# VectorE operations on two tiles at once, chained shifts and a different share of key tiles in a hand-scheduled attention block on one core

## The chip, the core and the metric

The kernel runs on one core of a Trainium2 chip. The core's engines are TensorE (PE, matmuls; its weight loads appear as PEld), VectorE (DVE), ScalarE (ACT), GpSimd (POOL) and SyncE (SP), which here only starts DMAs. The metric is the device time of one execution in microseconds (us); lower is better.

## The reference

```python
B, S, D, H = 1, 2048, 448, 16          # Dh = 28
qkv = (x @ wqkv).reshape(B, S, 3, H, Dh).transpose(2, 0, 3, 1, 4)
q, k, v = qkv[0], qkv[1], qkv[2]
scores = jnp.einsum("bhqd,bhkd->bhqk", q, k) * (Dh ** -0.5)
p = softmax(scores, axis=-1)
o = jnp.einsum("bhqk,bhkd->bhqd", p, v)
return o.transpose(0, 2, 1, 3).reshape(B, S, D) @ wo
```

All tensors are bfloat16. It is one multi-head self-attention block: projections, softmax(q k) v for 16 heads of 28 columns over 2048 positions, and an output projection.

## The kernel before

**Units and tiles.** The 16 heads are taken in four groups of four, the 2048 queries in four chunks of 512. A pair of group and chunk is a unit; there are 16. Inside a unit the keys come in 16 tiles of 128. For one unit, key tile and head the scores are a tile of 128 keys by 512 queries, one PSUM bank of float32. So there are 1024 score tiles. They come out of L911 (`s_one`): four heads lie in four row groups of 32 rows, so that matmuls of different heads can run side by side. The weighted sum over keys (L863, `pv_mm`) puts the four heads into four column groups of one accumulator bank; one pass over one key tile is four matmuls. An additional column of ones in the values yields the softmax's denominators. No maximum is subtracted; a check of the denominators at the end of the program (CK..., FLAG) chooses a general path (`_general`) if they leave a range.

**Two ways to an exponential.** The exponential is shared between two engines.

- *A tiles* go to ScalarE. Two score tiles form a group, held in banks 0 and 1 or, for the next group, 2 and 3. One ACTIVATE (L952) reads both and writes the bf16 weights into PT, a ring of 38 tiles. PE then makes one pass for each key tile (`pv_a`).
- *D tiles* go to VectorE. The score has been scaled so that one binary order is 1024 units. L972 (the operation named R) adds a constant, clips at zero and writes an int16, whose bits read as float16 are a piecewise linear version of the exponential. This first plane is written for four heads into PD[zs, 0]. Two shifted copies of it are made by L978 (H1, plus 341) and L980 (H2, plus 683), each an operation on 128x2048 int16 values. PE passes over all three planes with three differently weighted copies of the values (VC, factors TERM_C), three passes of four matmuls in place of one, and the sum of the three lines is much closer to the exponential (`pv_d`). PD has four slots (NZ = 4).

`D_COUNT` says for each unit how many of its 16 key tiles go to VectorE: 75 of 256 in all. `D_SETS` says which.

**Banks.** Banks 4 to 7 are a pool called M. From it come the accumulators of the units, the banks of projections, of output projections, and the banks of the D tiles, one for each. A D tile's bank is released by its R.

**Other work on the way.** The projections of keys, queries and values (L550, L572) are made while the units run and are evicted by VectorE (L532, L534). GpSimd writes the values and their weighted copies in place (L585, L591). When a unit is complete, `post_unit` evicts its accumulator to OTS (L730), takes the denominators through DRAM and back (L733 to L742), inverts them (L737), and GpSimd multiplies in four quarters of 128 queries (L747, `NM`), which puts the normalised output into QT. When all four head groups of a chunk are there, `out_proj` makes four output tiles (L698), evicts them (L712) and stores them by a DMA from SP (L714). The last unit has its own ending, `tail`: the first three head groups of its output projection are made ahead (L775, `PREOP`), the denominators are taken across partitions by small matmuls (L797, L810) instead of through DRAM, the fourth head group is added (L821), and four tiles are evicted, two by ScalarE (L824) and two by VectorE (L827), and stored (L829).

**Order.** All operations are first collected with their dependencies and a nominal duration. Then a planner (`_Prog.schedule`) simulates the engines once while the program is built and so fixes a static order for each engine: it takes the engine with the earliest possible start and, among the operations that can start within 150 ns, the one of the lowest `prio`. R has priority -90, evictions -95 to -100, shifts the running position. A D tile's score matmul rides along with the score matmuls of an A group if it can (`ride`, L156); otherwise it waits up to RIDE ns for it. `HOLD_BACK` lets a group's scores wait for a bank that comes free soon. On the chip every engine goes through its list in order, and an operation waits on semaphores for those that it depends on (`emit_engine`), also for those of its own engine. An operation that waits holds up everything behind it on its engine.

## Time and profile before

The median of five runs is 354.24 us (353.55 to 354.87). The profiled execution took 354.13 us; its span in the profile, first to last instruction, is 352.2 us.

| operation | line | count | mean ns of one |
|---|---|---|---|
| exponential of two A tiles, ScalarE | L952 | 362 | 1233 |
| R, one D tile, VectorE | L972 | 300 | 681 |
| H1, H2, one shift, VectorE | L978, L980 | 75 + 75 | 708, 712 |
| eviction of K and Q projections, VectorE | L534, L532 | 16 + 15 | 684, 685 |
| eviction of a unit's accumulator, VectorE | L730 | 15 | 681 |
| eviction of an output tile, VectorE | L712 | 12 | 611 |
| normalisation of 128 queries, GpSimd | L747 | 60 | 560 |

```profile
PE   7899999999999999999999999999999899999995
PEld 3333232223322232322322232332222222222223
DVE  1788999999999999999999998999999999999974
ACT  1899999999999999999999999999999999999991
```

How to read it: the span is cut into 40 equal slices, and each digit is the busy share of a slice in tenths, 9 being 90% or more. A mean duration contains latency that overlaps with the next instruction, so means times counts can be more than an engine's busy time. A row of a group ends with the idle time of the engine just before these instructions and what ended it. A chain row says when a stretch began, how long it took and which engine and line it was on. A row of waits reads: who waited for whom, us in total, times, longest.

### The profile page before, as it was taken

To read this page: it belongs to the slowest core of one execution; us is meant where nothing else is said; L and a number is where in the kernel's file an instruction comes from. 1 tells how busy PE (TensorE), PEld (TensorE's weight loads), DVE (VectorE), ACT (ScalarE), POOL (GpSimd) and SP (SyncE) were. 2 spreads that over 40 slices of the span, in tenths; PEclk is the share of its full clock that TensorE was granted. 3 is DMA by queue.
4 is the path that set the end of the run, shared out by engine and by line. 5 is a ranking of instruction groups with operands and counts; after the bars stand their busy time and mean duration, and the time that the engine had idled before them with its cause. 6 is when DMAs were issued, how large, how long until landed. Compare 5 with 4: busy or idle time off the path is not lost.

```text
span 352.2 us, 8543 instructions
## 1 busy us (share of the span) xinstructions
PE 333.0 (95%) x3601; PEld 98.1 (28%) x3601; DVE 328.7 (93%) x557; ACT 335.7 (95%) x367; POOL 69.4 (20%) x157
## 2 busy tenths in 40 slices
PE   7899999999999999999999999999999899999995
PEld 3333232223322232322322232332222222222223
DVE  1788999999999999999999998999999999999974
ACT  1899999999999999999999999999999999999991
POOL 7232031042042013104030130522220211010001
PEclk9999999999999999999999999999999999999999
DMA  9920010010101001010000101010010102030111
GB/s 160 215 54 2 13 38 5 4 32 3 29 10 33 0 4 33 0 32 6 21 13 3 34 0 27 10 33 1 5 32 4 32 17 70 4 85 13 41 34 57
DMA packets 21604, 10.63 MB, mean 30 GB/s; under 512 B 15676, under 2 KB 19516, under 8 KB 21560
## 3 DMA queue, kind: packets, MB, share of 16 engines
q1 hardware_dynamic: 20136, 9.71, 12.1%
q8 instruction: 30, 0.49, 0.6%
q10 hardware_dynamic: 1424, 0.31, 0.4%
q14 instruction: 14, 0.11, 0.1%
HBM read 5.83 MB, written 2.08 MB: 22 GB/s over the span
## 4 chain that ended last, share of the span: by engine, by line
ACT 79%; PE 9%; DVE 6%; DMA 4%; SPq 0%; issue 0%
ACT PT L952 79%; PE ps L911 3%; PE ps L863 3%; DVE PD L972 3%; DMA xT<-in_x_dram 2%; DVE PD L980 1%; DVE PD L978 1%; DMA LT<-scr_l 1%; PE ps L550 1%; PE ps L775 1%; DMA scr_l<-OTS 1%; SPq L459 0%; PE ps L821 0%; PE ps L810 0%; PE ps L698 0%
## 5 line engine op out<-in xcount | busy, mean ns | idle before, releaser
L952 ACT ACTIVATE PT<-ps 128x1024 bf16<-128x1024 f32 x362 | 332.6, 1233 | 1.8 <-PE ps L911 1.6
L972 DVE TENSOR_SCALAR PD<-ps 128x512 int16<-128x512 f32 x300 | 192.2, 681 | 7.7 <-PE ps L911 6.8
L911 PE MATMUL ps<-QT,KT 28*128 28x512 bf16 x1024 | 150.2, 384 | 10.9 <-ACT PT L952 8.9
L863 PE MATMUL ps<-PD,VC 128*32 128x512 f16 x900 | 80.1, 386 | 1.0 <-DVE PD L980 0.5
L911 PEld LDWEIGHTS ps<-QT,KT 28*128 28x128 bf16 x1024 | 38.5, 91 | 149.1 <-ACT PT L952 138.7
L863 PE MATMUL ps<-PT,V 128*32 128x512 bf16 x724 | 64.5, 385 | 0.7 <-DVE PD L972 0.4
L747 POOL TENSOR_TENSOR QT<-RB,OTS 128x128 bf16<-128x128 f32 x60 | 31.7, 560 | 165.7 <-DMA RB<-scr_r 165.7
L980 DVE TENSOR_SCALAR PD<-PD 128x2048 int16<-128x2048 int16 x75 | 53.4, 712 | 0.0
L978 DVE TENSOR_SCALAR PD<-PD 128x2048 int16<-128x2048 int16 x75 | 53.1, 708 | 0.1
L550 PE MATMUL ps<-xT,w_raw 128*32 128x512 bf16 x512 | 42.6, 385 | 1.8 <-DMA xT<-in_x_dram 1.2
L585 POOL TENSOR_SCALAR V<-VX 128x224 bf16<-128x224 f32 x32 | 12.7, 412 | 108.4 <-DVE VX L534 108.3
L863 PEld LDWEIGHTS ps<-PD,VC 128*32 128x32 bf16 x900 | 19.1, 94 | 32.8 <-issue 22.2
L863 PEld LDWEIGHTS ps<-PT,V 128*32 128x32 bf16 x724 | 15.7, 94 | 24.0 <-issue 20.7
L572 PE MATMUL ps<-w_raw,xT 128*128 128x112 bf16 x256 | 20.8, 215 | 0.0
L591 POOL TENSOR_SCALAR VC<-VX 128x112 bf16<-128x112 f32 (+1 forms) x48 | 19.1, 409 | 1.0
L572 PEld LDWEIGHTS ps<-w_raw,xT 128*128 128x128 bf16 x256 | 13.3, 98 | 10.8 <-issue 9.3
L550 PEld LDWEIGHTS ps<-xT,w_raw 128*32 128x32 bf16 x512 | 10.0, 94 | 19.9 <-issue 13.1
L698 PE MATMUL ps<-wop,QT 128*128 128x448 bf16 x48 | 13.5, 358 | 0.1
L534 DVE CAST KT<-ps 128x512 bf16<-128x512 f32 x16 | 10.9, 684 | 0.5 <-PE ps L550 0.3
L532 DVE TENSOR_SCALAR QT<-ps 128x512 bf16<-128x512 f32 x15 | 10.3, 685 | 0.3 <-PE ps L550 0.2
L730 DVE COPY OTS<-ps 128x512 f32<-128x512 f32 x15 | 10.2, 683 | 0.0
L534 DVE COPY VX<-ps 128x448 f32<-128x448 f32 x16 | 9.9, 617 | 0.1
(50 smaller groups left out, 50.6 us busy)
## 6 DMA issues: line engine op xcount, KB each, us to landing
RB<-scr_r SPq DMA_DIRECT2D x60, 64.0 KB, 2.0
out_dram<-OUTS SPq DMA_DIRECT2D x16, 112.0 KB, 1.7
w_raw<-in_wqkv_dram SPq DMA_DIRECT2D x3, 249.0 KB, 3.6
wop<-in_wo_dram SPq DMA_DIRECT2D x16, 24.5 KB
w_raw<-in_wqkv_dram ACTq DMA_DIRECT2D x3, 87.0 KB, 4.0
scr_l<-OTS SPq DMA_DIRECT2D x15, 8.0 KB
LT<-scr_l SPq DMA_DIRECT2D x15, 8.0 KB, 1.6
scr_r<-RS SPq DMA_DIRECT2D x15, 8.0 KB, 1.4
```

What stands on the lines that cost most here:

```text
L534: fe = (lambda e: e.tensor_copy(evac[0](), evac[1](hold[0].banks[0])))
L550: ins = e.matmul(ps[32 * h:32 * h + 32, b * 512:(b + 1) * 512], w_raw[:, wi(c, it), col:col + 32], xT[:, it, c * 512:(c + 1) * 512], start ...
L572: ins = e.matmul(ps[:, b * 512 + j * GD:b * 512 + (j + 1) * GD], xT[:, it, n * 128:(n + 1) * 128], w_raw[:, wi(c, it), 2 * D + g * GD:2 * ...
L591: sc = P.add("pool", (lambda e, dst=dst, j=j: e.tensor_scalar(dst, src, TERM_C[j], 1.0, ALU.mult, ALU.mult)), deps=[ev, ms_c1[j]], after=[ ...
L698: return e.matmul(bank(hold[0].banks[0])[:, 0:D], QT[:, gg, n * 128:(n + 1) * 128], wop[:, gg, :], start=(gg == 0), stop=(gg == G - 1))
L747: nm = P.add("pool", (lambda e, k=k: e.tensor_tensor(QT[:, g, c * QCH + k * w_:c * QCH + (k + 1) * w_], RB[:, ub, k * w_:(k + 1) * w_], OT ...
L863: return e.matmul(ps[32 * h:32 * h + 32, accb(u) * 512:(accb(u) + 1) * 512], lhsT, rhs, start=first, stop=False, skip_group_check=True, ti ...
L911: return e.matmul(bank(b), KT[32 * h:32 * h + DH, g, kt * 128:(kt + 1) * 128], QT[32 * h:32 * h + DH, g, c * QCH:(c + 1) * QCH], start=Tru ...
L952: ex = P.add("act", (lambda e, p0=p0, w=w, b0=b0: e.activation(PT[:, p0 * 512:(p0 + w) * 512], bank(b0, w), AF.Exp, scale=ESCALE)), deps=[ ...
L972: r = P.add("dve", (lambda e, hold=hold, zs=zs, h=h: e.tensor_scalar(PD[:, zs, 0, h * 512:(h + 1) * 512], bank(hold[0].banks[0]), ZBIAS, 0 ...
L978: h1 = P.add("dve", (lambda e, zs=zs: e.tensor_scalar(PD[:, zs, 1, :], PD[:, zs, 0, :], float(TERM_D[1]), None, ALU.add)), deps=rs_ + [z_l ...
L980: h2 = P.add("dve", (lambda e, zs=zs: e.tensor_scalar(PD[:, zs, 2, :], PD[:, zs, 0, :], float(TERM_D[2]), None, ALU.add)), deps=rs_ + [z_l ...
```

## The change

- *Pairs.* R gets a merge key "R" and the shifts a merge key "H". When the planner places one of them on VectorE and another with the same key could start within 40 ns, both become one `tensor_scalar` over an access pattern with one more dimension of two. Two Rs only fit if their banks are neighbours (`fits`). The planner counts the sum of both durations less 65 ns. Both banks are then released by the merged operation, and it waits for what either waits for.
- *Neighbours.* Where several M banks are free, the planner now prefers for a D tile one beside the last D tile's, and for other uses the outer banks 4 and 7.
- *Chained shifts.* H2 adds 341 to H1's plane, where it added 683 to the first plane. The factors and the constant in ZBIAS are changed to match.
- *Shares.* D_COUNT sums to 78 key tiles instead of 75, spread differently over the units; the last unit has 4 instead of 3, and its D tiles are placed over the first 85% of it.
- *Planes.* A PD plane's next writer waits for the passes over this plane and the next, instead of the first plane waiting for the last of the three passes.
- *Output projections.* Each output tile waits for its own quarter of GpSimd's multiplication, not for the last of the four. In the tail, the L775 matmuls of the third head group get an earlier priority, and the last of the four stores is issued by ScalarE instead of SP.
- *Planner's numbers.* Some latencies, durations, RIDE (12000 to 9000), HOLD_BACK (680 to 560) and the first projection's position.

```diff
+    def fits(self, mate):
+        return self.mkey != "R" or abs(self.rel[0][0].banks[0] - mate.rel[0][0].banks[0]) == 1
+
+    def merged(self, e, mate):
+        def pair(a, b):
+            return bass.AP(a.tensor, a.offset, [list(a.ap[0]), [b.offset - a.offset, 2]] + [list(d) for d in a.ap[1:]])
+        (o0, i0, args), (o1, i1, _) = self.pairs(), mate.pairs()
+        return e.tensor_scalar(pair(o0, o1), pair(i0, i1), *args)
...
+            mate = None
+            if op.mkey is not None:
+                near = [(start_of(k, free_t[e], True), k) for k in avail[e] if ops[k].mkey == op.mkey and op.fits(ops[k])]
+                near = [(a, k) for a, k in near if a <= st + self.MERGE_WAIT]
+                if near:
+                    a, k = min(near)
+                    mate = ops[k]
+                    avail[e].remove(k)
+                    st = max(st, a)
+                    op.t0 = st
+                    op.dur = op.dur + mate.dur - self.FIXED
+                    op.deps += [d for d in mate.deps if d not in op.deps]
+                    mate.alias = op
+                    mate.t0, mate.t1 = st, st + op.dur
+                    op.emit = (lambda a_, b_: lambda e_: a_.merged(e_, b_))(op, mate)
...
-                fr = sorted((v[0], b) for b, v in pools[pname].items() if not v[2])[:k]
+                fr = sorted((v[0], b) for b, v in pools[pname].items() if not v[2])
+                if k == 1 and pname == "M" and self.NEIGHBOURS:
+                    lim = max(fr[0][0], st - self.SYNC_LAT)
+                    held = {b: v[2] for b, v in pools[pname].items()}
+
+                    def worth(tb):
+                        b = tb[1]
+                        if op.ride:
+                            if abs(b - self.last_sd) == 1 and self.last_r is not None and self.last_r.t0 is None:
+                                return 0
+                            return 1 if any(held.get(n) is False for n in (b - 1, b + 1)) else 2
+                        return 0 if b in (min(held), max(held)) else 1
+                    fr = sorted((tb for tb in fr if tb[0] <= lim), key=lambda tb: (worth(tb), tb))
+                fr = fr[:k]
...
-TERM_D = (0, 341, 683)
-TERM_C = (2.671875, 2.125, 1.6875)
+TERM_D = 341
+TERM_C = (2.703125, 2.140625, 1.703125)
...
-D_COUNT = (4, 5, 6, 3, 5, 6, 4, 6, 4, 4, 5, 5, 5, 4, 6, 3)
+D_COUNT = (4, 5, 6, 4, 5, 6, 4, 6, 4, 5, 5, 5, 6, 4, 5, 4)
...
-                opm = P.add("pe", f_op, deps=[otn_ev[(gg, cc)]] + (([otn_ev[(g_, cc)] for g_ in range(G)] + dma_wo[-1:]) if gg == 0 else []),
+                opm = P.add("pe", f_op, deps=[otn_ev[(gg, cc)][n % NQT]] + (([otn_ev[(g_, cc)][n % NQT] for g_ in range(G)] + dma_wo[-1:]) if gg == 0 else []),
...
-                               kind="f", units=0.9, prio=(NU - PRE_LEAD if gg < 2 else T) + 0.1 * j + 0.01 * gg, name=f"PREOP{j}_{gg}", acq=("M", 1) if first and j < NQT - 1 else None)
+                               kind="f", units=0.86, prio=NU - PRE_LEAD + (0.0 if gg < 2 else 0.35) + 0.1 * j + 0.01 * gg, name=f"PREOP{j}_{gg}", acq=("M", 1) if first and j < NPM else None)
...
-                    outs_last[j] = P.add("sp", (lambda e, n=n, j=j: e.dma_start(of[n * 128:(n + 1) * 128, :], OUTS[:, j, :])), deps=[ev], after=[outs_last[j]],
-                                         dur=500, prio=T, name=f"ODMA{n}", dma_group=grp_out[j], nbytes=128 * D * 2)
+                    outs_last[j] = P.add("act" if j == NQT - 1 else "sp", (lambda e, n=n, j=j: e.dma_start(of[n * 128:(n + 1) * 128, :], OUTS[:, j, :])), deps=[ev], after=[outs_last[j]],
+                                         dur=500, prio=T, name=f"ODMA{n}", dma_group=grp_fin[j], nbytes=128 * D * 2)
...
-                r = P.add("dve", (lambda e, hold=hold, zs=zs, h=h: e.tensor_scalar(PD[:, zs, 0, h * 512:(h + 1) * 512], bank(hold[0].banks[0]), ZBIAS, 0.0, ALU.add, ALU.max)),
-                          deps=[sd, z_last[zs][0]], dur=600, prio=-90.0, name=f"R{bi}_{h}", rel=[(sd, 0)])
+                rp = (lambda hold=hold, zs=zs, h=h: (PD[:, zs, 0, h * 512:(h + 1) * 512], bank(hold[0].banks[0]), (ZBIAS, 0.0, ALU.add, ALU.max)))
+                r = P.add("dve", (lambda e, rp=rp: e.tensor_scalar(*rp()[:2], *rp()[2])),
+                          deps=[sd] + z_last[zs][0], dur=600, prio=-90.0, name=f"R{bi}_{h}", rel=[(sd, 0)])
+                r.mkey, r.pairs = "R", rp
...
-                    h1 = P.add("dve", (lambda e, zs=zs: e.tensor_scalar(PD[:, zs, 1, :], PD[:, zs, 0, :], float(TERM_D[1]), None, ALU.add)),
-                               deps=rs_ + [z_last[zs][1]], dur=600, prio=pos, name=f"H{bi}_1")
-                    h2 = P.add("dve", (lambda e, zs=zs: e.tensor_scalar(PD[:, zs, 2, :], PD[:, zs, 0, :], float(TERM_D[2]), None, ALU.add)),
-                               deps=rs_ + [z_last[zs][2]], after=[h1], dur=600, prio=pos, name=f"H{bi}_2")
+                    hs = []
+                    for j in (1, 2):
+                        hp = (lambda zs=zs, j=j: (PD[:, zs, j, :], PD[:, zs, j - 1, :], (float(TERM_D), None, ALU.add)))
+                        hs.append(P.add("dve", (lambda e, hp=hp: e.tensor_scalar(*hp()[:2], *hp()[2])),
+                                        deps=(rs_ if j == 1 else hs[:]) + z_last[zs][j], dur=600, prio=pos, name=f"H{bi}_{j}"))
+                        hs[-1].mkey, hs[-1].pairs = "H", hp
...
                     def mk(u=u, kt=kt, zs=zs, evs=evs):
+                        pd = [pv_d(u, kt, zs, j, evs[j]) for j in range(NTERM)]
                         for j in range(NTERM):
-                            op = pv_d(u, kt, zs, j, evs[j])
-                            z_last[zs][j] = op
-                        z_last[zs][0] = op
+                            z_last[zs][j] = pd[j:j + 2]
```

## The prediction

> **What bounds the kernel now.** I read the page's busy table and its chain of waits first, then the chain in order of time, then the timelines of VectorE and of the tail, then who waits for whom.

> ```profile
> PE 333.0 (95%) x3601; PEld 98.1 (28%) x3601; DVE 328.7 (93%) x557; ACT 335.7 (95%) x367; POOL 69.4 (20%) x157
> ...
> ACT 79%; PE 9%; DVE 6%; DMA 4%; SPq 0%; issue 0%
> ...
> L952 ACT ACTIVATE PT<-ps 128x1024 bf16<-128x1024 f32 x362 | 332.6, 1233 | 1.8 <-PE ps L911 1.6
> L972 DVE TENSOR_SCALAR PD<-ps 128x512 int16<-128x512 f32 x300 | 192.2, 681 | 7.7 <-PE ps L911 6.8
> ...
> L747 POOL TENSOR_TENSOR QT<-RB,OTS 128x128 bf16<-128x128 f32 x60 | 31.7, 560 | 165.7 <-DMA RB<-scr_r 165.7
> L980 DVE TENSOR_SCALAR PD<-PD 128x2048 int16<-128x2048 int16 x75 | 53.4, 712 | 0.0
> L978 DVE TENSOR_SCALAR PD<-PD 128x2048 int16<-128x2048 int16 x75 | 53.1, 708 | 0.1
> ```

> ScalarE's exponentials (L952) are the clock: 362 of them, back to back from 10.1 to 343.5 us, idle 1.8 us in between. But VectorE is 93% busy too and PE 95%: three engines are nearly full, so the chain's 79% on ScalarE doesn't say how soon the next one takes over. The chain in order of time shows that it sometimes does:

> ```profile
> 218.35 56.94 ACT PT L952 x62
> ...
> 278.29 1.86 DVE PD L972 x3
> 280.15 0.85 DVE PD L980
> 281.00 0.86 DVE PD L978
> 281.87 0.86 DVE PD L980
> 282.73 0.87 DVE PD L978
> 283.60 0.04 issue
> 283.64 0.62 PE ps L863 x8
> 284.26 0.34 PE ps L911 x3
> 284.60 0.02 issue
> 284.62 44.20 ACT PT L952 x48
> ```

> At 283 us PE stood at a shifted pass that VectorE had not delivered, the next scores came late behind it, and the exponentials stopped. The chain is on VectorE like this in two places, 197 to 217 us and 276 to 284 us, 6% of the span. For VectorE's prices:

> ```profile
> 110.36 3.07 DVE L972 TENSOR_SCALAR PD<-ps 128x512 int16<-128x512 f32 x5
> 113.35 0.68 DVE L532 TENSOR_SCALAR QT<-ps 128x512 bf16<-128x512 f32 x1
> 113.95 0.68 DVE L978 TENSOR_SCALAR PD<-PD 128x2048 int16<-128x2048 int16 x1
> 114.55 2.47 DVE L972 TENSOR_SCALAR PD<-ps 128x512 int16<-128x512 f32 x4
> ```

> Five score tiles take 3.07 us and the fifth ends 0.68 after it began, so one follows another by 0.60 us, not by the 681 ns of the page, which overlap. A shift also takes 0.60 (113.95 to 114.55). The four shifts of 0.86 in the chain are those that ran beside GpSimd's L747.

> [...] I use 0.067 as what one merged pair saves. [...]

> **The change, part by part,** against the profiled execution (354.13 us, span 352.2, so 1.9 around it; the median of the five runs is 354.24).

> *Three key tiles move from ScalarE to VectorE.* D_COUNT sums to 75 before and 78 after. Each key tile is four score tiles, so ScalarE has 1024 - 4x78 = 712 of them in 356 groups instead of 362. First to last exponential started in 332.0 us, 0.920 each; taking out the stops (about 3.6 us in all, counted over the pitches above 0.925) leaves 0.910. Six fewer: **-5.46 us**, as long as ScalarE stays the clock.

> *VectorE gets more.* 12 more score tiles and 6 more shifts at 0.60: +10.8. Between its first score tile (10.1) and its last shift's end (341.6), 331.5 us, VectorE's work is 300x0.598 + 150x0.60 + 5.5[...] + 47 evictions of projections (27.0) + 15 of accumulators (9.0) + 12 of outputs (6.4) + reciprocals and checks (3.6) = 321, and about 10 us are idle. After it: 321 + 10.8 = 331.8 without merging, in a stretch that should shrink to 326.

> *Merging gives back 0.067 a pair.* At most 156 + 78 = 234 pairs, 15.7 us. How many there are is the unknown. I counted over the timelines of before: at about a third of the starts of L972 (106 of 300) a second score tile was already finished, and 113 pairs of L972 stand next to each other on VectorE; at 113 of the 150 shift starts a second shift would have been ready even with the chained order. Not all pairs lie in neighbouring banks, though the change prefers such banks. I take 85 pairs of score tiles and 65 of shifts, 150 in all: -10.0. Ends: 80 pairs (-5.4) and 200 (-13.4). So the work is 321.8 and 4.2 us of idle time are left of 10. About 2.7 of that is idle in the first 40 us, where nothing can be merged in. VectorE therefore has almost no slack: a stop like that at 283 us gets likelier. Stops cost 3.6 us now; I add 0.9 (ends: -0.5, because queues of shifts drain faster, and +3).

> *Chained shifts.* The second shift now waits for the first on its own engine. A shift lasts 0.685 and its follower starts after 0.60, so an adjacent pair could cost some 0.09: at most 78x0.09 = 7 us if always adjacent; score tiles and the other batch's shifts lie between, and merged operations remove the adjacency, so I put it inside the 0.9. Behind the waiting shift stand score tiles, and PE waits for those (L911 weight loads, 4.0 us).

> *PE.* Each moved tile is three passes of four matmuls instead of one. Late in the chain a period reads 0.37 of scores and 0.55 of eight matmuls, so two such slots per exponential. Used now: 181 + 225 passes, 128 of projections, 128 of values and outputs, 662 of 724 slots; after it 668 of 712. From 91% to 94%, hidden under ScalarE, unless VectorE delays it.

> *Freed earlier.* A PD plane is released after the passes that read it, not after the batch's last; the projections' positions, the planner's latencies and HOLD_BACK shift the order by fractions of a period. Nothing (0.3 either way, inside the stops).

> *Tail.* From the last exponential to the end are 8.8 us.

> ```profile
> 346.46 0.74 PE L775 MATMUL ps<-wop,QT 128*128 128x448 bf16 x3
> ...
> 347.35 0.28 PEld L775 LDWEIGHTS ps<-wop,QT 128*128 128x128 bf16 x2
> ...
> 348.12 2.07 SPq L829 DMA_DIRECT2D out_dram<-OUTS  x4
> ...
> 348.62 0.62 DVE L827 CAST OUTS<-ps 128x448 bf16<-128x448 f32 x1 [0.25 <-PE ps L821]
> ```

> Four stores leave on SP one after another, 348.1 to 349.8, but the last eviction was over at 349.24. With the last store on ScalarE's queue it starts then, and the third store on SP, near 349.24, ends the kernel: -0.5. On ScalarE's queue it stands behind the third tile's eviction, which is over before, and only the closing branch is behind it. Five L775 matmuls run among the final ones at 346.5 and 347.5, because all waited for the last of GpSimd's four quarters (345.1); each now waits for its own, worth up to -0.9. Against it, unit 15 shrinks from 26 to 24 groups, so unit 14's normalisation, started by its eviction at 333.3, may come 1.8 us later relative to the end. I take 0 for this pair (ends -0.9, +0.8).

> Sum: 354.13 - 5.46 + 0.9 - 0.5 = 349.07; the median lies 0.1 above the profiled run: **349.2**.

> **Rivals.**

> *VectorE becomes the bound* (20%). With 100 pairs its stretch is 321 + 10.8 - 6.7 + 4 idle = 329.1 against 331.5, so -2.4, tail -0.5: 351.3. For it: 10 us of idle is all that it has. Against: the many ready shifts.

> *Slower: a double tile holds two banks* (14%). One mechanism at L972: a merged operation releases its first bank 0.53 us later. Of four rotating banks one belongs to the accumulator and often one to a projection, so two are left for scores, and scores are only issued with the next group, 0.92 us on. If half of 85 pairs miss a group, that is 39 us of late tiles; if a fifth finds no shift to fill in, VectorE idles 8 us more: 321 + 10.8 - 10 + 4 + 8 = 333.8, +2.3, tail -0.5: 356.0. It decides from some 6 us of added idle on. For it: L972 already waits 6.8 us for scores. Against: 18 waits only, and half of VectorE's other work can fill.

> *The merging does little* (3%): 40 pairs, 321 + 10.8 - 2.7 + 4 = 333.1, +1.6 - 0.5: 355.3. [...]

> *Better* (8%): the early L775 gain comes whole and stops fall by 0.5: 354.1 - 5.46 - 1.4 - 0.5 = 346.8.

> **The numbers.** My case, 55%, 349.2, its own range 347.6 to 350.9. A measurement here tells 0.2%, 0.7 us, from no change. Faster: 55 + 8 + 19 of the first rival's 20 = 82%; same 4%; slower 14%. The range 346.8 to 353.2 leaves out the slower cases (17%) and an edge of the best.

> **What would show it.** After: L952 x356 with its pitch near 0.92; L972 and the shift lines split into single and double forms, doubles near 1.13 us apart and 150 pairs; VectorE at 97 to 99% between 40 and 330 us; the chain more often on VectorE; SP with three last stores. Wrong if ScalarE's idle time or the pitch grows by over 3 us, if L972's wait for scores passes 12 us, or if a double shift lasts over 1.3 us away from GpSimd.

## The result and the profile after

The changed kernel takes **352.82 us** (median of 28 runs, 350.23 to 357.21); the kernel before takes 354.21 (49 runs, 353.34 to 354.88). The ratio is 0.9953, 95% interval 0.9942 to 0.9965. So it is faster by 0.5%, some 1.4 us, where the prediction had 5.0. The direction and the wide range (346.8 to 353.2) held; the size did not, and the range of the main case (347.6 to 350.9) was missed. The profiled execution took 351.67 us.

The page of the kernel after (engines, clock by slice, chain, and costliest groups; L1033 answers to L952 of before, L992 to L911, L1054 to L972, L944 to the PD and PT matmuls; L66 is the helper that emits merged operations):

```profile
span 349.9 us, 8617 instructions
PE 338.2 (97%) x3697; PEld 101.3 (29%) x3697; DVE 327.1 (93%) x440; ACT 331.2 (95%) x361; POOL 74.2 (21%) x157
PEclk9999999996999999999999999999999999999999
ACT 68%; PE 28%; DMA 2%; issue 1%; SPq 0%; DVE 0%
L1033 ACT ACTIVATE PT<-ps 128x1024 bf16<-128x1024 f32 x356 | 328.0, 1131 | 3.6 <-PE ps L992 2.3
L1054 DVE TENSOR_SCALAR PD<-ps 128x512 int16<-128x512 f32 x172 | 112.5, 681 | 4.7 <-PE ps L992 4.2
L66 DVE TENSOR_SCALAR PD<-ps 128x1024 int16<-128x1024 f32 x70 | 85.2, 1217 | 4.2 <-PE ps L992 3.9
L66 DVE TENSOR_SCALAR PD<-PD 128x4096 int16<-128x4096 int16 x65 | 79.8, 1230 | 0.0
```

The parts that the change is about are there: 356 exponentials, 70 double score tiles and 65 double shifts. Double tiles follow one another by 1.134 us, double shifts by 1.132 (medians), where two single ones need 1.196 and 1.200. What was not expected stands in the line of the clock, a 6 in the tenth slice. (The chain's 28% of PE, 9% before, is no sign of it: experiment 3 below has 33% at full clock.) From the first exponential's start to the last one's end took 333.38 us before (10.10 to 343.48) and 331.09 after (10.09 to 341.18). The stops between exponentials (the part of each pitch over 0.919, counted for pitches over 0.925) sum to 3.64 before and 7.48 after. What six exponentials gave, 5.46, was mostly taken back by 3.84 of new stops; the rest of the time, 0.909 us an exponential where it was 0.911, gave the other 0.67.

The timeline of the kernel after around that slice (start, duration, engine, line, operation; in brackets the idle time before it and what ended it):

```profile
74.52 0.39 PE L992 MATMUL ps<-QT,KT 28*128 28x512 bf16 x2 [0.53 <-ACT PT L1033]
...
75.61 4.69 ACT L1033 ACTIVATE PT<-ps 128x1024 bf16<-128x1024 f32 x5 [1.15 <-PE ps L944]
76.69 0.39 PE L992 MATMUL ps<-QT,KT 28*128 28x512 bf16 x2 [1.15 <-ACT PT L1033]
79.04 1.04 PE L944 MATMUL ps<-PD,VC 128*32 128x512 f16 x8
80.66 1.02 ACT L1033 ACTIVATE PT<-ps 128x1024 bf16<-128x1024 f32 x1 [0.36 <-PE ps L992]
```

And its windows (PE, PEld, DVE, ACT, POOL busy with counts, granted clock, DMA share, GB/s):

```profile
72.00:74.00 2.00, 1.99 (x26) 0.48 (x23) 2.00 (x4) 2.00 (x3) 0.47 (x2) 1.00 0.00 0
74.00:76.00 2.00, 1.02 (x10) 0.41 (x10) 2.00 (x4) 0.85 (x2) 0.00 (x0) 1.00 0.01 4
76.00:78.00 2.00, 1.28 (x14) 0.61 (x14) 1.01 (x2) 2.00 (x3) 0.00 (x0) 1.00 0.05 12
78.00:80.00 2.00, 1.99 (x16) 0.44 (x14) 1.72 (x2) 2.00 (x3) 0.00 (x0) 0.65 0.01 4
80.00:82.00 2.00, 2.00 (x19) 0.35 (x15) 1.26 (x2) 1.32 (x2) 1.78 (x5) 0.50 0.00 0
84.00:86.00 2.00, 2.00 (x22) 0.34 (x14) 0.76 (x2) 1.08 (x2) 0.00 (x0) 0.65 0.00 0
86.00:88.00 2.00, 2.00 (x28) 0.54 (x26) 2.00 (x3) 2.00 (x3) 0.00 (x0) 1.00 0.00 0
```

Read together: ScalarE starts an exponential at 73.25 and the next only at 75.61. Its bracket puts the 1.15 us down to PE's L944; but the PT matmuls of that line, whose buffer an exponential can wait for, were over at 73.61 (0.61 from 73.00), and PE in turn waits for ScalarE (0.53 and 1.15 us idle, released by L1033). Between them stands something that no group and no timeline shows. The trace's records of branches and instruction fetches do: a jump in ScalarE's own program at 73.12, and a fetch of 8192 bytes at 74.07. (Fetches on this queue follow the hints of other engines too: in the kernel before one at 53.52, after GpSimd's hint at 52.31. Which fetch is ScalarE's is judged from its time.) From 78.6 to 85.4 PE then runs at half clock (eight PD matmuls last 1.04 us; eight PT matmuls of the same size at full clock, 0.61), ScalarE waits for scores, and further pitches of 1.0 to 1.9 us follow. The stop itself is 1.44 us of excess, the stretch from 79 to 86 another 2.37: together 3.81 of the 3.84.

Where the jump stands is decided by these lines, which the change does not edit:

```python
        gap = {k: seq[k].t0 - seq[k - 1].t1 for k in range(1, len(seq))}
        jump = max((k for k in gap if self.JUMP_FROM <= seq[k].t0 < self.JUMP_TO), key=lambda k: gap[k])
        late = [k for k in gap if seq[jump].t0 - self.HINT_FIRST <= seq[k].t0 <= seq[jump].t0 - self.HINT_LAST]
        hint = max(late, key=lambda k: gap[k]) if late else jump - 1
```

ScalarE's program consists of two parts with the general path between them, so an unconditional jump leads from the first to the second. A hint, an instruction that names the jump's target, stands some exponentials ahead. `split` puts ScalarE's jump at the largest planned gap between 60 and 160 us. Before, all planned gaps there were zero, so the first place won: the jump before exponential 55 (E55, at 59.99 us), the hint before E48 (53.62), a fetch 1.24 us after the hint and no stop. In the re-planned order one gap of 4.6 ns appeared; the jump went before E70 and the hint before E63 (66.91), no fetch followed the hint in the next 2.7 us, and the fetch at 74.07 came 0.95 us after the jump.

The stop doesn't lead to the half clock in every execution, nor for the same length, so the time varies: the granted clock was 0.984 to 0.985 in 16 of 30 executions, 0.989 to 0.99 in 7, 0.994 to 0.995 in 5, 1.0 in one and 0.971 in one; before it is 0.997 to 1.0. Ratios leave out executions more than 1.5% slower than the kernel's fastest, medians don't, so where the clock varies a median can lie above its ratio.

### The profile page after: what moved, and what is told of

Same layout as the page of the kernel before. It is cut to its first block, busy times and chain, and to the rows that moved or that the text cites. A ratio compares the mean times of both kernels' runs of the same rounds, so it can differ in the third digit from the quotient of the medians.

```text
span 349.9 us, 8617 instructions
## 1 busy us (share of the span) xinstructions
PE 338.2 (97%) x3697; PEld 101.3 (29%) x3697; DVE 327.1 (93%) x440; ACT 331.2 (95%) x361; POOL 74.2 (21%) x157
## 4 chain that ended last, share of the span: by engine, by line
ACT 68%; PE 28%; DMA 2%; issue 1%; SPq 0%; DVE 0%
ACT PT L1033 68%; PE ps L992 11%; PE ps L944 10%; PE ps L774 2%; DMA xT<-in_x_dram 2%; PE ps L621 1%; PE ps L643 1%; PE ps L858 1%; SPq L530 0%; PE ps L902 0%; PE ps L891 0%; PE ps L878 0%; PE ps L935 0%; DVE OUTS L908 0%; DVE FLAG L1096 0%
## 5 line engine op out<-in xcount | busy, mean ns | idle before, releaser
L1033 ACT ACTIVATE PT<-ps 128x1024 bf16<-128x1024 f32 x356 | 328.0, 1131 | 3.6 <-PE ps L992 2.3
L992 PE MATMUL ps<-QT,KT 28*128 28x512 bf16 x1024 | 152.8, 388 | 4.7 <-ACT PT L1033 3.0
L1054 DVE TENSOR_SCALAR PD<-ps 128x512 int16<-128x512 f32 x172 | 112.5, 681 | 4.7 <-PE ps L992 4.2
L66 DVE TENSOR_SCALAR PD<-ps 128x1024 int16<-128x1024 f32 x70 | 85.2, 1217 | 4.2 <-PE ps L992 3.9
L944 PE MATMUL ps<-PD,VC 128*32 128x512 f16 x936 | 83.9, 390 | 1.5 <-DVE PD L66 1.1
L992 PEld LDWEIGHTS ps<-QT,KT 28*128 28x128 bf16 x1024 | 39.6, 91 | 141.8 <-ACT PT L1033 125.8
L66 DVE TENSOR_SCALAR PD<-PD 128x4096 int16<-128x4096 int16 x65 | 79.8, 1230 | 0.0
L944 PE MATMUL ps<-PT,V 128*32 128x512 bf16 x712 | 65.5, 389 | 0.5 <-DVE PD L1054 0.4
L656 POOL TENSOR_SCALAR V<-VX 128x224 bf16<-128x224 f32 x32 | 15.1, 490 | 150.2 <-DVE VX L605 150.2
L944 PEld LDWEIGHTS ps<-PD,VC 128*32 128x32 bf16 x936 | 19.9, 94 | 34.9 <-issue 22.8
L944 PEld LDWEIGHTS ps<-PT,V 128*32 128x32 bf16 x712 | 15.9, 94 | 25.2 <-issue 22.6
L662 POOL TENSOR_SCALAR VC<-VX 128x112 bf16<-128x112 f32 (+1 forms) x48 | 20.7, 442 | 1.0
L643 PE MATMUL ps<-w_raw,xT 128*128 128x112 bf16 x256 | 19.6, 214 | 0.0
L1064 DVE TENSOR_SCALAR PD<-PD 128x2048 int16<-128x2048 int16 x26 | 18.2, 708 | 0.1
L774 PE MATMUL ps<-wop,QT 128*128 128x448 bf16 x48 | 13.7, 357 | 0.1
```

Of the source, the lines that this page charges most:

```text
L66: return e.tensor_scalar(pair(o0, o1), pair(i0, i1), *args)
L643: ins = e.matmul(ps[:, b * 512 + j * GD:b * 512 + (j + 1) * GD], xT[:, it, n * 128:(n + 1) * 128], w_raw[:, wi(c, it), 2 * D + g * GD:2 * ...
L656: sc = P.add("pool", (lambda e, Vd=Vd, vs=vs: e.tensor_scalar(Vd, vs, 1.0, 1.0, ALU.mult, ALU.mult)), deps=[ev, ms_v1], after=[sc], dur=34 ...
L662: sc = P.add("pool", (lambda e, dst=dst, j=j: e.tensor_scalar(dst, src, TERM_C[j], 1.0, ALU.mult, ALU.mult)), deps=[ev, ms_c1[j]], after=[ ...
L774: return e.matmul(bank(hold[0].banks[0])[:, 0:D], QT[:, gg, n * 128:(n + 1) * 128], wop[:, gg, :], start=(gg == 0), stop=(gg == G - 1))
L944: return e.matmul(ps[32 * h:32 * h + 32, accb(u) * 512:(accb(u) + 1) * 512], lhsT, rhs, start=first, stop=False, skip_group_check=True, ti ...
```

## The experiments

The theory to test (A): the moved jump causes the stop, the stop the half clock, and without both the prediction's sum holds. Rivals: the merged operations or the denser PE work make the stop wherever the jump stands; the half clock has a cause of its own; or the gain of the six exponentials is not there at all.

**1. The jump alone, nearer.** After, with ScalarE's jump before E60 and the hint seven ahead.

```diff
         if e == "dve":
             return 0, 1
+        if e == "act":
+            k = next(k for k in range(len(seq)) if seq[k].name == "E60")
+            return k - 7, k
```

> The changed kernel with one thing moved: ScalarE's unconditional jump into its second code part stands before exponential E60 (about 64 us) instead of E70 (73.1 us); no arithmetic and no order changes. Theory A (after the jump ScalarE waits for an instruction fetch for over 1 us, PE then idles on it, and the idle stretch makes the PE clock drop to half [...]): the stop of 2.4 us at 73 us goes, the granted clock is 0.995 or more, the time is 349.0 (348.2 to 349.9), ratio to before 0.983 to 0.988. Rival B (PE and VectorE are too full with 78 key tiles and stop there whatever the jump does): clock stays at 0.985 to 0.99, 352 to 353, ratio 0.995.

Measured: 351.66 us (350.26 to 352.42), ratio 0.9924 [0.9903, 0.9944]. The stop did not go, it went along: jump at 63.78, fetch at 64.89, a pitch of 2.69 us at 63.9. So the stop belongs to the jump and not to what VectorE or PE do at 73 us; but my picture that an early place suffices was wrong. The clock was 0.995 or more in three of six executions, the profiled one among them.

**2. The jump moved in the kernel before.** The same lines with E70 in the kernel before, nothing else.

> The kernel before with ScalarE's jump moved from E55 (60.0 us) to E70 (about 74 us)[...]. Theory A: a stop of over 1 us appears behind the jump at 73 to 76 us, the clock drops below 0.995 in most runs, and the time rises by 1.2 to 4 us: 355.4 to 358.2, ratio 1.003 to 1.011. Rival B (the jump is harmless, the changed plan was the cause): no change, 354.2, ratio 1.000, clock 1.0.

Measured: 358.94 us (355.74 to 362.4), ratio 1.0105 [1.0066, 1.0145]. The median is a little above the expected range; the clock was below 0.995 in four of six executions. In the profiled one, the slowest (362.4 us), the jump is at 73.99, a fetch at 75.17, a pitch of 2.72 us at 74.0, and half clock from 79.0 to 99.5. Its clock by slice:

```profile
PEclk9999999985599999999999999999999999999999
```

No double operation, no chained shift and no moved tile is in this kernel: the place of the jump and its hint alone makes both the stop and the half clock.

**3. The jump where it was before.** After, with `"E55"` in the lines of experiment 1 (hint before E48).

> The changed kernel with ScalarE's hint and jump at the same exponentials as in the kernel before, hint before E48 (53 us) and jump before E55 (60 us). In the profiles a fetch of instructions came 1.2 us after this hint in the kernel before and ScalarE never stopped; behind hints at E53 and E63 (the changed kernel, E60, the kernel before with E70) no fetch came until 1.0 us after the jump, and ScalarE stopped for 1.1 to 1.8 us. Theory A2 (the late hint is lost, the fetch then stops ScalarE, and PE's idling costs clock): a fetch near 54.8 us, no stop at the jump, clock 0.996 or more, 348.8 us (348.2 to 349.6), ratio 0.983 to 0.987. Rival C (every jump of ScalarE stops it in the fuller plan, the place is no matter): a stop of over 1 us at 60 us, 350.2 to 352.5.

Measured: **348.25 us** (347.99 to 348.59), ratio 0.9834 [0.982, 0.9848], better than both kernels. The fetch comes at 54.09, before the jump, and the clock was 1.0 in every run. Its page:

```profile
span 346.6 us, 8617 instructions
PE 335.6 (97%) x3697; PEld 101.1 (29%) x3697; DVE 327.1 (94%) x440; ACT 330.8 (95%) x361; POOL 74.8 (22%) x157
PEclk9999999999999999999999999999999999999999
ACT 50%; PE 33%; DVE 13%; DMA 2%; issue 0%; SPq 0%
L1036 ACT ACTIVATE PT<-ps 128x1024 bf16<-128x1024 f32 x356 | 327.6, 1133 | 1.2 <-PE ps L995 0.9
```

Against the page of after: the same instructions, ScalarE's busy time the same within 0.4, but its waits 1.2 instead of 3.6 and no slice at a lower clock. The stops sum to 4.25 us. The chain is now on three engines.

**4. Place of the hint or distance to the jump?** After, with the jump before E70 as the change has it, but the hint before E48 (`k - 22`).

> The changed kernel with its own jump (before E70, 73 us), but the hint before E48 instead of E63, so 22 exponentials ahead instead of 7. Theory A2 in the form that the hint's place decides: as the jump at E55, 348.8 us (348.2 to 349.6), clock 0.996 or more, a fetch near 54.8 us. Rival D (the hinted instructions are lost again before the jump, or the jump's own place decides): the stop of over 1 us at 73 us stays, with half clock, 351.5 to 353.

Measured: 348.23 us (348.0 to 348.53), ratio 0.9833 [0.9819, 0.9847]. A fetch comes at 54.01, 1.24 us after the hint. Another comes at 74.10, 1.08 us after the jump (73.02), as one does in the kernel before (61.09), and ScalarE doesn't stop for it. With a fetch after its hint the jump at E70 costs nothing that shows: 348.23 here, 348.25 with the jump at E55.

**5. The same distance at another place.** `"E75"` and `k - 22`, so the hint before E53.

> The changed kernel with the hint before E53 and the jump before E75, 22 exponentials apart as in the run with E48 and E70. If the hint's place decides: no fetch 1.2 us after the hint, a stop of over 1 us at 78 us, 350.2 to 353. If the distance decides: no stop, 348.3.

Measured: 350.73 us (350.08 to 351.25), ratio 0.9916 [0.99, 0.9933]. No fetch after the hint (57.88), jump at 77.75, fetch at 78.95, a pitch of 2.80 us. Twenty-two exponentials were not enough here, so the distance does not decide; in all 14 kernels the outcome goes with the place of the hint. Why hints before E53 and E63 bring no fetch stays open. The kernels in which they fail show another fetch near 44 us that those with a working hint lack; I did not test whether that is the cause.

**6. Stop without half clock.** After with its own jump, and seven more filler passes of PE (zero weights, so no value changes) behind the stop.

```diff
+        more = {"S72": 2, "S73": 5}.get(nxt.name, 0)
+        op.fill += more
+        if more:
+            op.fill_unit = live[-1]
         spare = nxt.t0 - op.t1 - 20.0
```

> The changed kernel with its own hint and jump, and 2 and 5 more passes of zero weights into the open accumulator (the kernel's own filler, adding nothing) in PE's queue in front of the scores of groups 72 and 73, where PE stood idle for 0.5 and 1.2 us. Theory A (two separate costs: the fetch stops ScalarE, and PE's idling then drops the clock): the stop at 73 us stays at 1.0 to 1.5 us, the clock is 0.996 or more in most runs, 350.3 us (349.7 to 351.2). Rival E (the drop of the clock doesn't come from PE's idling there): clock 0.985 to 0.99 and 352.5 to 353.2.

Measured: 350.9 us (350.65 to 351.28), ratio 0.9909 [0.9895, 0.9923], clock 1.0 in all runs. Its windows:

```profile
74.00:76.00 2.00, 1.59 (x22) 0.53 (x18) 2.00 (x4) 0.60 (x2) 0.00 (x0) 1.00 0.04 12
76.00:78.00 2.00, 1.24 (x22) 0.62 (x18) 1.27 (x3) 2.00 (x3) 0.00 (x0) 1.00 0.01 4
78.00:80.00 2.00, 2.00 (x30) 0.74 (x22) 0.31 (x1) 1.33 (x2) 0.00 (x0) 1.00 0.00 0
80.00:82.00 2.00, 2.00 (x25) 0.53 (x23) 2.00 (x3) 2.00 (x3) 0.47 (x2) 1.00 0.01 4
```

ScalarE's stop is still there (0.60 busy of 2.00), the clock stays at 1.00. This splits the loss: 352.82 - 350.9 = 1.9 us are the half clock, 350.9 - 348.25 = 2.65 the stop and what follows it at full clock. The added passes may cost something themselves: the one execution of the unaltered changed kernel at clock 1.0 took 350.23 us, which splits the loss into 2.6 and 2.0.

**7. What the six exponentials are worth.** After, jump before E55, with 75 key tiles on VectorE instead of 78. A first try with the jump before E60 and the list of before had the stop (64.1), half clock (68.2 to 88.7) and other shares for the last two units:

> The changed kernel with the jump at E60 and the shares of before (D_COUNT sums to 75, 362 exponentials), merging kept. If ScalarE is the clock, six exponentials at 0.91 us come back: e1's time plus 5.2 to 5.6 less any stops that a relaxed VectorE saves (before had 3.6 us of stops): 353.2 (351.5 to 354.5), ratio 0.995 to 1.000. Rival (the gain is in the merging and the new order themselves, not in the share): within 2 us of e1.

Measured: 363.25 us (358.3 to 365.07), ratio 1.0165 [1.012, 1.0211], from which the share of the tiles can't be told. Repeated with three units changed and the last two left alone:

```diff
-D_COUNT = (4, 5, 6, 4, 5, 6, 4, 6, 4, 5, 5, 5, 6, 4, 5, 4)
+D_COUNT = (4, 5, 6, 3, 5, 6, 4, 6, 4, 4, 5, 5, 5, 4, 5, 4)
```

> The changed kernel with hint and jump as before (E48, E55) and three key tiles given back to ScalarE (units 3, 9 and 12; 75 in all, units 14 and 15 as in the change), merging kept (94 pairs). If ScalarE is the clock, six more exponentials at 0.91 us: 348.25 + 5.5 = 353.7 (352.7 to 354.3), granted clock 0.996 or more. Rival (merging and the new order bring part of the gain by themselves): 350 to 352.

Measured: 353.27 us (352.67 to 354.91), ratio 0.9981 [0.9966, 0.9997], clock 0.998 to 1.0. That is 5.0 us over experiment 3: six exponentials cost nearly their full 5.46. It also says that the rest of the change without the three tiles is worth about 0.2% (the last two units keep the shares 5 and 4 of the change; they were 6 and 3).

**8. No merging.** After, jump before E60, `near = [...]` replaced by `near = []`.

> The changed kernel with the jump at E60 and no merging (78 key tiles on VectorE, neighbour banks and chained shifts kept, all 312 R and 156 shifts single). If VectorE is the next bound, as my sum had it (331.8 us of work and 4 idle in place of 331.5): 358 (355.5 to 361), with VectorE 99% busy between 100 and 300 us and the chain on VectorE. Rival (there was enough slack, merging brings little): 350 to 352.

Measured: 367.09 us (364.8 to 373.39), ratio 1.0338 [1.0299, 1.0376]. That is above the expected range. The profiled execution is the slowest (373.39 us): the clock is half from 275.7 to 306.4, and 15.1 us instead of 8.7 pass between the last exponential and the end. But two executions at a clock of 0.994 and 0.995 still took 365.56 and 364.8. VectorE was busy for 95% of 100 to 300 us, not 99, and has 22% of the chain, PE 47%. The kernel also has the stop of experiment 1, so the next two merge one kind each with the jump before E55.

**9. Only score tiles merged** (`if op.mkey == "R":`), 59 pairs.

> The changed kernel with hint and jump as before (E48, E55) and only score tiles merged (59 pairs, no merged shifts). VectorE gets 76 operations back that cost 0.067 us each, 5.1 us. If VectorE is the bound next to ScalarE: 353.5 us (352 to 356), between e5 and the kernel without pairs. Rival (only the doubled shifts matter, or VectorE had slack): 349 to 350.

Measured: 366.73 us (361.65 to 381.05), ratio 1.0235 [1.0207, 1.0264]. Windows of the profiled execution (370.12 us):

```profile
260.00:280.00 20.00, 19.11 (x149) 4.08 (x145) 17.15 (x24) 16.57 (x18) 3.04 (x4) 0.63 0.02 4
280.00:300.00 20.00, 19.61 (x143) 3.88 (x135) 15.30 (x21) 15.46 (x17) 2.14 (x4) 0.69 0.07 15
```

Far above what I expected. VectorE and ScalarE, both full elsewhere, are at 76 to 86%, PE is full at a clock of 0.63 to 0.69: once it is slow, PE is what the others wait for. Most of the loss is not the clock, though: two executions at 0.991 and 0.990 took 361.65 and 363.34 us, 13 and 15 above experiment 3. In the profiled one ScalarE also stands for 4.2 us at 302.4 at full clock, in a wait put down to PE's L947, and 14.5 us pass from the last exponential to the end.

**10. Only shifts merged** (`if op.mkey == "H":`), 73 pairs.

> The changed kernel with hint and jump as before and only shifts merged (73 pairs, no merged score tiles). VectorE gets 62 operations back that cost 0.067 us each, 4.2 us. If stops and PE's clock multiply what VectorE lacks, as without shift pairs (366.7 for 5.1 us more work): 352 to 360, with the clock below 0.995. Rival (linear: the added work alone): 350 to 352.5.

Measured: 357.57 us (356.86 to 359.01), ratio 1.0118 [1.009, 1.0147], clock 1.0 in three of four executions. The time lies in the first range, but PE's clock, which I had given as the reason, is not it: here VectorE is late. Its timeline at the end:

```profile
342.19 1.22 DVE L66 TENSOR_SCALAR PD<-PD 128x4096 int16<-128x4096 int16 x1
...
345.97 0.69 DVE L1067 TENSOR_SCALAR PD<-PD 128x2048 int16<-128x2048 int16 x1
```

The last exponential ends at 341.4 (337.9 in experiment 3), but shifts run to 346.7 (336.6), and 13.7 us pass to the end instead of 8.7. Seventy pairs of score tiles fewer and eight of shifts more are 70 x 0.062 - 8 x 0.068 = 3.8 us of work at what a pair saves in the kernel after (the 4.2 expected took 0.067, my estimate); the span grew by 8.4. From 300 to 340 us VectorE is busy for 39.06 us (37.53 in experiment 3): there its slack is used up, as the rival of the prediction had it. Over the whole it is not: between its first score tile and its last shift's end it idles 9.0 us, mostly in waits for scores (6.7).

**11. The last store back on SP.** Experiment 3 with `"act" if j == NQT - 1 else "sp"` replaced by `"sp"`.

> The changed kernel with hint and jump as before and the last of the four closing stores issued by SP again. If the queue on SP holds the last store back as it did before (0.5 us in my prediction): 348.25 + 0.5 = 348.75 (348.5 to 349.0). Rival (the end is set elsewhere): 348.2.

Measured: 349.1 us (348.71 to 349.58), ratio 0.9866 [0.985, 0.9883]: 0.85 us slower than experiment 3. The last store in this run, and in experiment 3:

```profile
343.65 1.84 SPq L913 DMA_DIRECT2D out_dram<-OUTS  x4
344.31 0.38 ACTq L913 DMA_DIRECT2D out_dram<-OUTS  x1
```

Counted from the last exponential's end, the last store is issued at 6.60 us here and at 6.38 in experiment 3, and the span ends at 8.89 and 8.70. So only 0.19 of the 0.68 us between the two profiles lie where the store is. The rest lies before the first exponential (it starts at 10.39 for 10.08) and among the exponentials; what makes it is not known.

## Why the prediction was right in direction and wrong in size

- **The step that failed** is the term for stops, "+0.9 (ends -0.5, +3)". It measured +3.84 in the profiled run, and so met my own sign of being wrong (over 3 us). I priced in it only stops that VectorE causes, put PE "hidden under ScalarE", and put the planner's new order at "Nothing (0.3 either way, inside the stops)". What I overlooked is that a new plan also moves what the planner places by its gaps: ScalarE's jump. No part of the diff names it, but `split` reads `self.order`, which the change alters. Then the cover was gone: PE stood 0.53 and 1.15 us behind ScalarE and dropped to half clock, which it could not absorb (the 94% of used slots is my estimate): from 80 to 86 us it was busy all 6.00 us, at a clock of 0.55, and ScalarE for 4.16. Experiments 2, 4 and 6 show both halves.
- **With the hint at work the sum holds.** Experiment 3 has 348.25 against 349.2. Its stops grew by 0.6 (4.25 - 3.64), inside the 0.9. The time between the stops gave 0.67 that was not in my sum, and the tail gave 0.4 less than I had counted: that the two offset each other in part is luck.
- **Six exponentials, -5.46:** right; 5.0 by experiment 7. ScalarE is the clock, as long as VectorE keeps up.
- **Pairs:** 135 instead of 150 (70 of scores for 85, 65 of shifts as taken). Each saves 0.062 or 0.068, by pitch, for the 0.067 taken: 70 x 0.062 + 65 x 0.068 = 8.8 us instead of 10.0. The 0.067 was my estimate, which no run had shown. The trace of before gives one near it: the next operation starts 0.531 us after an output tile of 448 columns (L712) and 0.598 after a score tile of 512, and a line through both leaves 0.062 for the operation itself. A merged shift, 4096 columns in 1.132 us, is no slower a column than single ones, 2 x 0.600; no row of before spoke for that.
- **VectorE as the bound (351.3, 20%):** did not happen with both kinds merged: in experiment 3 VectorE still idles 5.7 us between its first score tile and the last shift's end (8.1 before). With one kind it was late at the end (experiment 10), at a higher price than I gave the rival, since VectorE's lag also lengthens the end. (Of the chain from 197 to 217 us before, which I read as VectorE's, 5.3 us are DMA, from 210.9 to 216.2. The 5.5 in my sum of VectorE's work was an estimate for shifts beside GpSimd: before, 20 shifts last over 0.70 us, all beside L747, L585 or L591, and together 3.9 us more than at the usual 0.685.)
- **A double tile holds two banks (356.0, 14%):** not seen, though a double tile does last 0.54 us longer (1.217 for 0.681). The waits for scores are 4.2 + 3.9 = 8.1 us in single and double form after, 6.8 before, under the 12 that I had named as the sign.
- **Tail, -0.5:** -0.07 in the profiled run (8.70 us from the last exponential to the end, 8.77 before), and again two parts offset each other. From the last eviction's end to the end 2.36 us pass instead of 3.00. But the last eviction ends 6.34 us after the last exponential instead of 5.76. Of the first part, experiment 11 puts 0.19 down to the store; I had read the third store of the kernel before as leaving SP near 349.24, but it left at 349.38. The second part, +0.58, lies inside the +0.8 that I allowed. The timeline of after at the end:

```profile
343.32 1.71 POOL L825 TENSOR_TENSOR QT<-RB,OTS 128x128 bf16<-128x128 f32 x4 [20.46 <-DMA RB<-scr_r]
344.37 1.12 PE L858 MATMUL ps<-wop,QT 128*128 128x448 bf16 x5
...
346.90 0.62 DVE L908 CAST OUTS<-ps 128x448 bf16<-128x448 f32 x1 [0.25 <-PE ps L902]
347.56 0.38 ACTq L910 DMA_DIRECT2D out_dram<-OUTS  x1
```

GpSimd's four quarters of unit 14 start 2.1 us after the last exponential's end; before they started 0.1 ahead of it. That is the late normalisation of my sum, 2.2 us for the 1.8 that I had. But its start does not set the end: in the profiles of after and of experiments 3, 4 and 11 the quarters start 2.15, 2.17, 2.39 and 1.82 us after the last exponential, and the last eviction ends at 6.34 or 6.35 in all four. In all four, five L858 matmuls (1.12 us) stand in PE's order ahead of L902, where three L775 (0.74 us) stood before. So letting each wait for its own quarter did not take them out of the end. That this order makes the 0.58 is read from the traces; no run isolates it.

## What to carry to other kernels

When an edit makes a planner order the work anew, list everything that is placed by that order, not only the work: jumps, hints and fillers move too, and the page's groups show none of them. A ScalarE stop of 1.4 us cost 2.0 to 2.65, and 1.9 to 2.6 more through PE's clock, so look at the clock line first when a gain is missing, and then at the records of fetches where a bracket names a releaser that was long done. With two engines both at 93 to 95%, a saving on one is only cashed while the other's slack lasts: the merging is worth little by itself, but it is what pays for the moved tiles.

## What the runs showed of the hardware that was not expected

```profile
75.17:78.58 3.41, 2.22 (x28) 1.10 (x24) 2.14 (x4) 2.97 (x4) 0.00 (x0) 1.00 0.03 7
80.36:83.77 3.41, 2.06 (x28) 0.64 (x28) 1.97 (x3) 3.14 (x4) 0.38 (x1) 1.00 0.01 2
272.25:275.66 3.41, 3.41 (x33) 1.04 (x33) 3.27 (x6) 3.36 (x4) 0.00 (x0) 1.00 0.01 2
```

What decides stays open. The half clock lasted 6.8, 20.5, 20.5, 27.3 and 30.7 us in five profiled runs (2, 6, 6, 8 and 9 such stretches), though PE was nearly always busy in it (6.83 of the 6.83 us in after, 3.40 of 3.40 in the first and in the last such stretch of experiment 2).
